# Half of a first MoE layer as seven-product Strassen units, in a kernel of chunked attention followed by a two-layer MoE

## The chip, the cores and the metric

The kernel runs on one core of one Trainium2 chip. The metric is the device time of one execution in microseconds (us). Executions come with the span from first to last instruction, which is about 1.8 us shorter than the time, and with the mean granted clock of the matrix engine (1.0 is full speed). In the text, PE is the matrix engine, PEld its weight loads, DVE the vector engine, ACT the activation engine and POOL the general engine, which here also issues the loads of q, k and v.

## The reference, cut to what matters

```python
def _attn_ref(q, k, v):                  # q, k, v: (8, 8, 576, 64), float32
    # chunks of 64 rows; softmax(q k^T / 8) v inside each chunk
    ...
    return out

def _moe_ref(x, w_in, w_out, beta):      # x: (4608, 512), w_in: (512, 2048), w_out: (2048, 512)
    h = x @ w_in                         # first layer
    g = h * (1.0 / (1.0 + np.exp(-beta * h)))
    return (g @ w_out).astype(np.float32)   # second layer
```

The attention's output, with the heads laid side by side, is the x of the MoE. The kernel computes in 16-bit floats with 32-bit accumulation.

## The kernel before

Tokens go through in nine blocks of 512. Block 0 is treated apart. In the others (1 to 8) the first layer makes sixteen tiles of h ("m-tiles", 128 features by 512 tokens). Each is four matmuls of 128x512 into one PSUM bank, and one Silu on ACT which writes the f16 array `gt`:

```python
    def emit_h(j, m, c0=0, c1=BLK):
        ...
        for n in range(KDM):                      # KDM = 4
            e, z = n // 2, n % 2
            nc.tensor.matmul(
                out=hps_t[j, m][:, c0:c1],
                lhsT=w_r[m // 4][:, 2 * z + e, m // 2 % 2, m % 2, :],
                rhs=xt_t[j][:, n, c0:c1],
                start=(n == 0), stop=(n == KDM - 1),
            )

    def emit_g(j, m):
        hps = hps_t.pop((j, m))
        nc.scalar.activation(
            out=gt_t[j][:, m, :], in_=hps, func=ACTF.Silu,
            scale=beta2[:, m % 2, m // 2:m // 2 + 1],
        )
```

The second layer already is one Strassen step of seven products. Its sums over `gt` (s1 and s2 on DVE, s3 on POOL) are made while the first layer still runs:

```python
    def L1(j, hooks={}, nh=2):
        ...                                       # tiles 0 and 1 first, in two halves
        for m in range(nh, KFF):                  # KFF = 16
            hooks.get(m, lambda: None)()
            emit_m(j, m)                          # emit_h, emit_g
            if j == 0:
                continue
            if m == 8:
                for p in range(4):
                    emit_sum(j, 3, p)             # POOL, needs tiles 0 to 7 only
            if m in (9, 11, 13, 15):
                p = (m - 9) // 2
                fill.extend([lambda w=w, p=p: emit_sum(j, w, p) for w in (1, 2)])
            if m >= 10 and j > 1:
                dve()                             # takes one sum from fill
        hooks.get(KFF, lambda: None)()            # the next block's first scores
```

The steps of the second layer (`mm`) are mixed with the next block's attention (`at`) and with transposes of later q and k (`tr`). At the end of a block POOL is given the loads of a later block, so they run in the following block's first layer:

```python
            mm[5]()
            if j < NB - 1:
                cC()
            go(tr)
            mm[6]()                               # ends with a PSUM copy on ACT and an add on POOL
            if j + 2 < B:
                load_v(j + 2)                     # four loads issued by POOL
            if j + 3 < B:
                load_qk(j + 3)                    # two more
```

Once, before block 1, the weights w_out are scaled and four combinations of them (`tw`) are formed on POOL:

```python
        scale_w_out(0)
        scale_w_out(1)
        for f in T_items(1):                      # transposes of q and k
            f()
        scale_w_out(2)
        scale_w_out(3)
        emit_tw(1)
        emit_tw(2)
        load_v(2)
        load_qk(3)
        emit_tw(4)
        emit_tw(3)
```

Each engine takes its instructions in the order in which the program lists them, and that order is what this case is about: in e4 below, a changed order on ACT alone takes away a wait of 2.62 us.

The softmax here doesn't subtract the row's maximum and nothing guards it: scores larger than these inputs give would overflow.

## Time and profile before

| | before |
|---|---|
| time, median of 3 (lowest to highest) | 289.00 us (288.88 to 289.02) |
| profiled span, granted clock | 287.1 us, 0.999 |
| block 4: first layer with scores / second layer | 14.70 / 14.30 us |
| length of blocks 2 to 7 | 28.97 to 29.00 us |

The length of a block here and below runs from the first matmul of its first layer to the first one of the next block's. "First layer" runs up to the first product of the second layer.

The page of the profiled execution gives the span, the busy time of each engine with its share of the span and its number of instructions, the granted clock in tenths for 40 slices, and the chain of waits that ended last:

```profile
span 287.1 us, 7722 instructions
...
PE 271.6 (95%) x3388; PEld 176.4 (61%) x3388; DVE 140.6 (49%) x261; ACT 161.8 (56%) x240; POOL 117.1 (41%) x114
...
PEclk9999999999999999999999999999999999999999
...
PE 82%; DMA 10%; DVE 3%; POOL 2%; issue 1%; ACT 1%; DVEq 0%; POOLq 0%; ACTq 0%
...
```

PE is busy 95% of the time at full clock, and 82% of the chain is PE. The timeline of PE for one steady block (block 4) gives start, duration, engine, line of the program, operation, output and inputs, shapes and count; a bracket would give idle time before the group and who ended it:

```profile
...
141.39 14.12 PE L240 MATMUL hps<-xt,wi 128*128 128x256 f16 x72
155.44 0.71 PE L155 MATMUL sc<-qT,kT 32*64 32x64 f16 x64
156.09 1.92 PE L310 MATMUL oA<-w_out,gt 128*128 128x256 f16 x16
...
170.39 1.80 PE L240 MATMUL hps<-xt,wi 128*128 128x256 f16 x14
```

There is no bracket: from 141.39 to 170.39 us PE goes from one product to the next. ACT in the same block:

```profile
...
142.24 1.28 ACT L250 ACT_TABLE_LOAD   x1
143.53 3.21 ACT L250 ACTIVATE gt<-hps,beta 128x512 f16<-128x512 f32 x5
...
```

ACT loads the table of the Silu, then does the first five Silus, which had piled up, in one go. POOL in the same block:

```profile
...
143.52 3.44 POOL L95 DMA_DIRECT2D vb<-in_v_dram  x4
...
147.61 0.77 POOL L85 DMA_DIRECT2D ku<-in_k_dram  x1
148.33 4.73 POOL L274 TENSOR_TENSOR s<-gt 128x512 f16<-128x512 f16 x4
```

POOL issues six loads from 143.52 us on, and only after the last of them, at 148.33, starts the sums s3: 4.81 us. Nothing on PE waits for this. The windows view gives for each stretch its length, the busy time of PE, PEld, DVE, ACT and POOL (instructions in brackets), the granted clock, and the DMA's share and rate:

```profile
...
core 0: us, PE busy (x) PEld busy (x) DVE busy (x) ACT busy (x) POOL busy (x), PEclk, DMA share, GB/s
141.39:156.09 14.70, 14.70 (x139) 7.48 (x136) 5.17 (x8) 12.40 (x18) 10.77 (x11) 1.00 1.19 160
156.09:170.39 14.30, 14.30 (x249) 12.05 (x242) 10.61 (x20) 5.26 (x9) 1.27 (x1) 1.00 0.37 74
...
```

In the first layer PE has no free time, ACT is busy 12.40 of 14.70 us, POOL 10.77 and DVE 5.17.

### The profile page before, as it was taken

The page shows a single profiled execution, that of the slowest core. Times are in us where ns is not written, and L with a number is a line of the kernel's source. Part 1 is how long each engine was busy: PE and PEld are TensorE (multiplying, and loading weights), DVE is VectorE, ACT ScalarE, POOL GpSimd, SP SyncE. Part 2 cuts the span into 40 slices and gives each one's busy share as a digit, 9 for nine tenths or more (in the row PEclk, how much of TensorE's full clock was granted, in tenths as well). Part 3 has the DMA queues.
Part 4 walks back from the last instruction along what each step waited for, and adds up shares of the span by engine and source line. Part 5 has one row for each costly group of instructions (what it writes and reads, how often), then busy time and mean ns, then how long its engine had stood idle before and what let it go on. Part 6 is the DMA issues. An engine that isn't in the chain of part 4 may idle for free.

```text
span 287.1 us, 7722 instructions
## 1 busy us (share of the span) xinstructions
PE 271.6 (95%) x3388; PEld 176.4 (61%) x3388; DVE 140.6 (49%) x261; ACT 161.8 (56%) x240; POOL 117.1 (41%) x114
## 2 busy tenths in 40 slices
PE   2779978999999999999999999999999999999995
PEld 0454434546874688468845884588458845885584
DVE  2751483837770677067806680668055404540433
ACT  2249505688348833883388438842884288518710
POOL 8733266994049203920393039302910260016100
PEclk9999999999999999999999999999999999999999
DMA  6999998990239626972597259823902320242013
GB/s 112 177 206 212 211 182 153 184 211 3 75 110 158 130 67 112 159 132 63 105 161 142 59 99 164 154 59 94 154 4 57 94 73 2 57 94 73 2 37 110
DMA packets 69584, 31.95 MB, mean 111 GB/s; under 512 B 53680, under 2 KB 63920, under 8 KB 69552
## 3 DMA queue, kind: packets, MB, share of 16 engines
q0 software_dynamic: 44960, 18.35, 51.9%
q1 hardware_dynamic: 24448, 12.99, 17.4%
q8 instruction: 26, 0.43, 0.6%
q10 hardware_dynamic: 144, 0.13, 0.1%
q14 instruction: 6, 0.05, 0.1%
HBM read 36.71 MB, written 9.44 MB: 161 GB/s over the span
## 4 chain that ended last, share of the span: by engine, by line
PE 82%; DMA 10%; DVE 3%; POOL 2%; issue 1%; ACT 1%; DVEq 0%; POOLq 0%; ACTq 0%
PE hps L240 39%; PE oA L310 20%; DMA ku<-in_k_dram 7%; PE oD L310 5%; PE oB L310 5%; PE oC L310 5%; PE sc L155 4%; PE x L183 3%; DMA vb<-in_v_dram 3%; PE ops L405 1%; DVE kT L127 1%; DVE w_out L118 1%; POOL qu L85 1%; PE oE L310 1%; POOL vb L95 1%
## 5 line engine op out<-in xcount | busy, mean ns | idle before, releaser
L240 PE MATMUL hps<-xt,wi 128*128 128x512 f16 (+1 forms) x656 | 127.8, 353 | 1.2 <-DMA wi<-in_moe_w_in_dram 0.7
L250 ACT ACTIVATE gt<-hps,beta 128x512 f16<-128x512 f32 x144 | 95.8, 688 | 17.8 <-PE hps L240 17.1
L240 PEld LDWEIGHTS <-wi 128*128 128x128 f16 x656 | 63.4, 98 | 61.7 <-DMA xt<-x 1.5
L270 DVE TENSOR_TENSOR s<-gt 128x512 f16<-128x512 f16 x32 | 17.7, 552 | 80.1 <-ACT gt L250 79.9
L355 POOL TENSOR_TENSOR w<-u,u 128x512 f32<-128x512 f32 x7 | 8.9, 1270 | 103.3 <-ACT u L321 103.3
L310 PEld LDWEIGHTS <-s 128*128 128x128 f16 x496 | 46.8, 98 | 6.0
L310 PE MATMUL oA<-tw,s 128*128 128x256 f16 x368 | 44.1, 273 | 0.0
L274 POOL TENSOR_TENSOR s<-gt 128x512 f16<-128x512 f16 x32 | 37.5, 1228 | 4.8 <-ACT gt L250 4.8
L310 PEld LDWEIGHTS <-gt 128*128 128x128 f16 x384 | 36.4, 98 | 4.8
L321 ACT COPY u<-oA 128x512 f32<-128x512 f32 x24 | 14.1, 588 | 37.0 <-PE oA L310 37.0
L164 ACT ACTIVATE et<-sc 128x512 f16<-128x512 f32 x34 | 18.5, 595 | 22.3 <-PE sc L155 22.2
L95 POOL DMA_DIRECT2D vb<-in_v_dram x32 | 27.5, 879 | 6.6 <-DMA wi<-in_moe_w_in_dram 5.0
L200 DVE TENSOR_TENSOR x<-x,rd 128x512 f16<-128x512 f32 x34 | 23.5, 691 | 1.3
L127 DVE STREAM_TRANSPOSE qT<-qu 128x576 f32<-128x576 f32 x16 | 20.0, 1250 | 5.8 <-DMA qu<-in_q_dram 5.8
L127 DVE STREAM_TRANSPOSE kT<-ku 128x576 f32<-128x576 f32 x16 | 19.9, 1241 | 2.1 <-DMA ku<-in_k_dram 2.0
L155 PEld LDWEIGHTS <-kT 32*64 32x64 f16 x1152 | 11.6, 111 | 12.2 <-DVE kT L127 6.3
L155 PE MATMUL sc<-qT,kT 32*64 32x64 f16 x1088 | 12.8, 195 | 6.2 <-DVE kT L127 5.4
L272 DVE TENSOR_TENSOR s<-s,gt 128x512 f16<-128x512 f16 x32 | 17.8, 555 | 1.1
L372 ACT COPY o<-oA 128x512 f32<-128x512 f32 x7 | 4.1, 586 | 23.2 <-PE oA L310 23.2
L405 PE MATMUL ops<-w_out,gt 128*128 128x512 f16 x64 | 15.3, 379 | 1.5 <-DVE w_out L118 1.5
L375 POOL TENSOR_TENSOR o<-t,o 128x512 f32<-128x512 f32 x7 | 8.9, 1270 | 18.0 <-ACT o L372 18.0
L164 ACT ACT_TABLE_LOAD x8 | 10.3, 1283 | 10.0 <-PE sc L155 9.9
(56 smaller groups left out, 208.8 us busy)
## 6 DMA issues: line engine op xcount, KB each, us to landing
out_dram<-osb SPq DMA_DIRECT2D x21, 256.0 KB, 2.2
vb<-in_v_dram POOLq DMA_DIRECT2D x32, 144.0 KB, 4.9
qu<-in_q_dram POOLq DMA_DIRECT2D x7, 576.0 KB, 9.1
ku<-in_k_dram POOLq DMA_DIRECT2D x7, 576.0 KB, 11.1
out_dram<-o SPq DMA_DIRECT2D x14, 256.0 KB, 2.2
wi<-in_moe_w_in_dram POOLq DMA_DIRECT2D x4, 512.0 KB, 12.5
w_out<-in_moe_w_out_dram POOLq DMA_DIRECT2D x4, 512.0 KB, 16.8
qu<-in_q_dram POOLq DMA_DIRECT2D x2, 288.0 KB, 5.3
```

Of the source, the lines that this page charges most:

```text
L95: nc.gpsimd.dma_start(out=t[64 * hp:64 * hp + 64, 2 * z:2 * z + 2, :, 0:D].rearrange("p s c d -> p (s c) d"), in_=v[b, h0:h0 + 2].rearrang ...
L127: nc.vector.transpose(out=dst[b][:, z].rearrange("p t r e -> p (t r e)").bitcast(FP32).rearrange("p (t r) -> p r t", r=RUN), in_=src[b][:, ...
L155: nc.tensor.matmul(out=sc[a % 2][o0:o0 + 64, z, c, :], lhsT=kk[:, cb * CH:(cb + 1) * CH, e], rhs=qq[:, cb * CH:(cb + 1) * CH, e], start=(e ...
L164: nc.scalar.activation(out=et, in_=sc[s], func=ACTF.Exp, scale=scale)
L200: nc.vector.tensor_tensor(out=yy, in0=src, in1=rr.to_broadcast(shape), op=ALU.mult,)
L240: nc.tensor.matmul(out=hps_t[j, m][:, c0:c1], lhsT=w_r[m // 4][:, 2 * z + e, m // 2 % 2, m % 2, :], rhs=xt_t[j][:, n, c0:c1], start=(n == ...
L250: nc.scalar.activation(out=gt_t[j][:, m, :], in_=hps, func=ACTF.Silu, scale=beta2[:, m % 2, m // 2:m // 2 + 1],)
L270: tt(out=s1[:, lo], in0=g[:, lo, dn], in1=g[:, hi, dn], op=ALU.add)
L272: tt(out=s2[:, lo], in0=s1[:, lo], in1=g[:, lo, up], op=ALU.subtract)
L274: tt(out=s3[:, lo], in0=g[:, lo, up], in1=g[:, lo, dn], op=ALU.subtract)
L310: nc.tensor.matmul(out=bank[name][:, i, :], lhsT=a[:, kk, i * 128:(i + 1) * 128], rhs=b[:, kk, :], start=(first and i == 0 and kk == 0), s ...
L405: nc.tensor.matmul(out=ops[t], lhsT=gt_t[j][:, kk, t * 128:(t + 1) * 128], rhs=wo(kk), start=(kk == 0), stop=(kk == KFF - 1),)
```

## The change

The intent is to take matmul time away where PE has no gap. A *unit* makes four of the sixteen m-tiles (2q, 2q+1, 4+2q, 5+2q) by the Strassen-Winograd scheme, with w_in quarters A11..A22 and token-block quarters B11..B22. It has seven products of four 128x256 matmuls: 28 of 256 columns stand for 16 of 512, 12.5% less work. Two units make tiles 0 to 7. Between their products stand the plain tiles 8 to 15 as "spacers", meant to hide the combining of sums. PE accumulates several products in one PSUM bank, so intermediate values are copied out before the next product is added:

- bank A: A11·B11 → copy u1 (ACT); + S2·T2 → copy u2 (DVE); + S3·T3 → copy u3 (DVE); + A22·T4 gives one quarter of the result
- bank C: S1·T1 → copy w1 (DVE); + S4·B22, plus u2 (DVE) gives a second quarter
- bank B: A12·B21, plus u1 (DVE) gives a third
- t = u3 + w1 on POOL gives the fourth

Six Silus then close the unit. The f16 sums T1..T4 of the tokens (`xs`) are made on DVE at the start of every block. The memory for this comes from `gt`, which is left with one buffer. The diff, cut to its core:

```diff
-    gt_p = ctx.enter_context(tc.tile_pool(name="gt", bufs=2))
+    gt_p = ctx.enter_context(tc.tile_pool(name="gt", bufs=1))
...
+    def emit_xs(j):
+        ...
+        tt(out=t[0], in0=b12, in1=b11, op=ALU.subtract)
+        tt(out=t[1], in0=b22, in1=t[0], op=ALU.subtract)
+        tt(out=t[2], in0=b22, in1=b12, op=ALU.subtract)
+        tt(out=t[3], in0=b21, in1=t[1], op=ALU.subtract)
+
+    def unit(j, q, spacers):
+        ...
+        prod("A", a11, b11, True)
+        snap("u1", "A", "a")                      # copy on ACT
+        spacers[0]()
+        prod("A", swr[1], ts[1], False)
+        snap("u2", "A", "v")                      # copy on DVE
+        prod("C", swr[0], ts[0], True)
+        snap("w1", "C", "v")
+        spacers[1]()
+        prod("A", swr[2], ts[2], False)
+        snap("u3", "A", "v")
+        sb["t"] = u_p.tile([128, 2, HT], FP32, tag="t", name="t")
+        nc.gpsimd.tensor_tensor(out=sb["t"], in0=sb["u3"], in1=sb["w1"], op=ALU.add)
+        prod("B", a12, b21, True)
+        nc.vector.tensor_tensor(out=c1[:, :, up_], in0=bank["B"], in1=sb["u1"], op=ALU.add)
+        spacers[2]()
+        prod("A", a22, ts[3], False)
+        prod("C", swr[3], b22, False)
+        nc.vector.tensor_tensor(out=c1[:, :, dn_], in0=bank["C"], in1=sb["u2"], op=ALU.add)
+        for i in range(2):
+            silu(m2 + i, dn_, sb["t"][:, i])
+        for i in range(2):
+            silu(m2 + i, up_, bank["A"][:, i])
+        for i in range(2):
+            silu(m1 + i, slice(0, BLK), c1[:, i])
...
+    def L1(j, hooks={}, first=None):              # blocks 1 to 8
+        ...
+        emit_xs(j)
+        unit(j, 0, [sp(8), sp(9), sp(10)])
+        sp(11)()
+        for p in (0, 2):
+            emit_sum(j, 3, p)
+        unit(j, 1, [sp(12), sp(13), sp(14)])
+        for p in (1, 3):
+            emit_sum(j, 3, p)
+        sp(15)()
...
         scale_w_out(1)
-        for f in T_items(1):
-            f()
+        T1 = T_items(1)
+        T1[0]()
+        T1[1]()
         scale_w_out(2)
+        T1[2]()
+        T1[3]()
         scale_w_out(3)
+        load_v(2)
         emit_tw(1)
+        load_qk(3)
         emit_tw(2)
-        load_v(2)
-        load_qk(3)
```

Left out are the making of the weight sums `sw`, some extra idle matmuls at the start, and a moved hook. In block 1 the four transposes T2 move to tiles 9, 11, 13 and 15.

More of the change, by code (lines that the diff above doesn't have):

```diff
@@ L51 @@
     xt_p = ctx.enter_context(tc.tile_pool(name="xt", bufs=2))
-    gt_p = ctx.enter_context(tc.tile_pool(name="gt", bufs=2))
+    gt_p = ctx.enter_context(tc.tile_pool(name="gt", bufs=1))
     s_p = ctx.enter_context(tc.tile_pool(name="s", bufs=1))
     u_p = ctx.enter_context(tc.tile_pool(name="u", bufs=1))
+    xs_p = ctx.enter_context(tc.tile_pool(name="xs", bufs=1))
+    c_p = ctx.enter_context(tc.tile_pool(name="c", bufs=2))
     osb_p = ctx.enter_context(tc.tile_pool(name="osb", bufs=4))
@@ L70 @@
     tw = [big.tile([128, NM, HM], FP16, name=f"tw{i}") for i in range(4)]
+    sw = [big.tile([128, 2, DFF // 4], FP16, name=f"sw{i}") for i in range(4)]
     NV = 3
@@ L220, in emit_xp, with emit_idle @@
         nc.scalar.copy(out=xt_t[j][:, :, t0:t0 + 128], in_=xps)
-    def emit_idle(n):
+    def emit_idle(n, w=512):
         d = ps_p.tile([128, BLK], FP32, tag="p", name="idle")
         for _ in range(n):
-            nc.tensor.matmul(out=d, lhsT=zero[:, 0:128], rhs=zero, start=True, stop=True)
+            nc.tensor.matmul(
+                out=d[:, 0:w], lhsT=zero[:, 0:128], rhs=zero[:, 0:w], start=True, stop=True)
     gt_t = {}
@@ L253, in emit_g, with emit_sw @@
         )
+    xs_t = {}
+    def emit_sw():
+        s1, s2, s3, s4 = sw
+        a11, a12 = w_in16[0][:, 0::2], w_in16[0][:, 1::2]
+        a21, a22 = w_in16[1][:, 0::2], w_in16[1][:, 1::2]
+        tt = nc.vector.tensor_tensor
+        tt(out=s1, in0=a21, in1=a22, op=ALU.add)
+        tt(out=s2, in0=s1, in1=a11, op=ALU.subtract)
+        tt(out=s3, in0=a11, in1=a21, op=ALU.subtract)
+        tt(out=s4, in0=a12, in1=s2, op=ALU.subtract)
+    def emit_xs(j):
+        x = xt_t[j]
+        b11, b12 = x[:, 0:2, 0:HT], x[:, 0:2, HT:BLK]
+        b21, b22 = x[:, 2:4, 0:HT], x[:, 2:4, HT:BLK]
+        t = xs_t[j] = [xs_p.tile([128, 2, HT], FP16, tag=f"xs{i}", name=f"xs{i}") for i in range(4)]
+        tt = nc.vector.tensor_tensor
+        tt(out=t[0], in0=b12, in1=b11, op=ALU.subtract)
+        tt(out=t[1], in0=b22, in1=t[0], op=ALU.subtract)
+        tt(out=t[2], in0=b22, in1=b12, op=ALU.subtract)
+        tt(out=t[3], in0=b21, in1=t[1], op=ALU.subtract)
@@ new lines, in unit, with prod, snap, silu @@
+    def unit(j, q, spacers):
+        x = xt_t[j]
+        ts = xs_t[j]
+        up_, dn_ = slice(0, HT), slice(HT, BLK)
+        b11, b21, b22 = x[:, 0:2, up_], x[:, 2:4, up_], x[:, 2:4, dn_]
+        swr = [t.rearrange("p k (m i r) -> p k m r i", r=2, i=128) for t in sw]
+        a11, a12, a22 = w_r[0][:, 0::2], w_r[0][:, 1::2], w_r[1][:, 1::2]
+        bank = {"A": ps_s.tile([128, 2, HT], FP32, tag=f"sc{q}", name="wA")}
+        xx = ps_x.tile([128, 2, 2, HT], FP32, tag="x", name="wX")
+        bank["B"], bank["C"] = xx[:, 0], xx[:, 1]
+        sb = {}
+        def prod(b, a, rhs, first):
+            for i in range(2):
+                for kk in range(2):
+                    nc.tensor.matmul(
+                        out=bank[b][:, i, :], lhsT=a[:, kk, q, i, :], rhs=rhs[:, kk, :],
+                        start=(first and i == 0 and kk == 0), stop=(kk == 1),
+                        skip_group_check=True,
+                    )
+        def snap(nm, b, eng):
+            sb[nm] = u_p.tile([128, 2, HT], FP32, tag=nm, name=nm)
+            if eng == "a":
+                nc.scalar.copy(out=sb[nm], in_=bank[b])
+            else:
+                nc.vector.tensor_copy(out=sb[nm], in_=bank[b])
+        def silu(m, cols, src):
+            nc.scalar.activation(
+                out=gt_t[j][:, m, cols], in_=src, func=ACTF.Silu,
+                scale=beta2[:, m % 2, m // 2:m // 2 + 1],
+            )
+        m1, m2 = 2 * q, 4 + 2 * q
+        c1 = c_p.tile([128, 2, BLK], FP32, tag="c1", name="c1")
+        prod("A", a11, b11, True)
[20 more added lines that the diff above has]
+            silu(m2 + i, up_, bank["A"][:, i])
+        for i in range(2):
+            silu(m1 + i, slice(0, BLK), c1[:, i])
@@ L433, in dve, with L1_plain @@
                 fill.pop(0)()
-    def L1(j, hooks={}, nh=2):
+    def L1_plain(j, hooks, nh):
         for m in range(nh):
@@ L442, in L1, with sp, f @@
         for m in range(nh, KFF):
-            hooks.get(m, lambda: None)()
             emit_m(j, m)
-            if j == 0:
-                continue
-            if m == 8:
-                for p in range(4):
-                    emit_sum(j, 3, p)
-            if m in (9, 11, 13, 15):
-                p = (m - 9) // 2
-                fill.extend([lambda w=w, p=p: emit_sum(j, w, p) for w in (1, 2)])
-            if m >= 10 and j > 1:
-                dve()
+    def L1(j, hooks={}, first=None):
+        gt_t[j] = gt_p.tile([128, KFF, BLK], FP16, tag="gt", name="gt")
+        def sp(m):
+            def f():
+                hooks.get(m, lambda: None)()
+                emit_m(j, m)
+            return f
+        if first:
+            first()
+        emit_xs(j)
[7 more added lines that the diff above has]
+        sp(15)()
+        for p in (0, 2, 1, 3):
+            fill.extend([lambda w=w, p=p: emit_sum(j, w, p) for w in (1, 2)])
+        dve(4)
         hooks.get(KFF, lambda: None)()
@@ L500 @@
         emit_pv(1, spare=True, xbar=False)
+        emit_idle(4, 256)
         emit_xp(0)
@@ L504 @@
         emit_pv(3, spare=True, xbar=False)
-        L1(0, {-2: lambda: emit_xp(2), -3: lambda: emit_xp(3)}, 4)
+        L1_plain(0, {-2: lambda: emit_xp(2), -3: lambda: emit_xp(3)}, 4)
+        emit_sw()
         scale_w_out(0)
         scale_w_out(1)
-        for f in T_items(1):
-            f()
+        T1 = T_items(1)
+        T1[0]()
+        T1[1]()
         scale_w_out(2)
+        T1[2]()
+        T1[3]()
         scale_w_out(3)
+        load_v(2)
         emit_tw(1)
+        load_qk(3)
         emit_tw(2)
-        load_v(2)
-        load_qk(3)
         emit_tw(4)
@@ L520 @@
             9: lambda: emit_sc(2),
-            11: lambda: emit_sc(3),
-            12: lambda: emit_pv(4, xbar=False),
+            12: lambda: [emit_pv(4, xbar=False), emit_sc(3)],
             13: lambda: [emit_pv(5, xbar=False), emit_xp(4)],
@@ L537 @@
                 T2 = T_items(2)
-                hooks.update({-1: lambda: emit_xp(7), 4: T2[0], 7: T2[1], 10: T2[2], 12: T2[3]})
-            L1(j, hooks)
+                hooks.update({9: T2[0], 11: T2[1], 13: T2[2], 15: T2[3]})
+            L1(j, hooks, (lambda: emit_xp(7)) if j == 1 else None)
             at = []
```

## The prediction

> **What bounds the kernel now.** PE is 95% busy on the page; the chain of waits is 82% PE. In the timeline the steady token block (141.56 to 170.55 us) is unbroken matmuls: first layer 13.95 us, second layer with attention 15.05. In the first-layer window ACT is busy 11.86 us, DVE 5.00, POOL 10.77.
>
> **What the change removes.** In the chain, 128x512 matmuls cost 218 ns and 128x256 ones 109 ns. A unit replaces 16 of 512 (3.49 us) by 28 of 256 (3.06 us). Two units save 0.86 us per block, 6.9 over eight: 282 us if nothing else changed. Splitting the w_out scaling should remove PE's 1.5 us wait at 41.3 us: about 2 with nearby waits.
>
> **What it adds, per block.** ACT: two copies (0.59 us) and, per unit, four 256-wide Silus where two 512-wide ones stood. [...] DVE: four f16 additions (0.42 us alone), ten PSUM operations (0.69). POOL: two additions (1.27).
>
> **The new chain.** ACT and PE are in order, so I laid each engine's instructions out in issue order with these durations (an estimate; the same layout of the present kernel gives 29.1 us per steady block, trace 28.99). From the first-layer start T:
> 1. ts1 is ready only near T+2.5: DVE transposes until T+1.2, and the f16 additions stretch beside POOL's output addition (0.97 to 1.26 us in this trace[...]). PE waits about 1.3 us in unit 0.
> 2. t of unit 0 queues on POOL behind the v, q and k load issues, until T+6.9, and ends near T+8.1. ACT waits for it, then runs six Silus and tile 11's before unit 1's u1 copy, near T+12.2. Unit 1's second product may not overwrite that bank before: PE waits about 3 us (2 in blocks without loads).
> 3. The scores then wait for A's Silus, the second layer for the last c1 Silu: 1.4 us.
>
> Net: 5.8 us of waits less 1.4 us of saved or absorbed PE work: +4.3 us in blocks 2 to 5, +3 in 6 to 8. In block 1 the four 4.1 us POOL subtractions for tw run until about 58 us and hold up the f16 additions: +4 to +7. The single g buffer costs nothing: its readers end before the next Silu. Sum: +31, less 2 for w_out.
>
> **Prediction:** 319 us, 306 to 329 eight times in ten. Faster by over 2%: 0.03; within 2%: 0.03; slower by over 2%: 0.94.
>
> **What would show it.** PE busy falls to about 85%. The timeline shows one PE gap of 2 to 3.5 us per block ended by ACT u1 in unit 1, one near 1 us ended by DVE ts and smaller ones before scores and the second layer. First-layer windows are 17 to 19 us, second-layer ones stay 15. The POOL t additions start right after load issues.
>
> **What would make it wrong.** t issued earlier than the loads, half Silus much faster than estimated, or unblocked DVE additions: then the loss shrinks towards 290. If gaps slow later matmuls, worse than 329.

Its sum is +31 less 2 on the 289 us of before, which was put at 319. The trace of before has no 256-wide Silu, and of the additions only their times, 0.97 and 1.26 us beside POOL's sums and 0.41 to 0.43 after them (block 4). The steps to T+12.2 and to the wait of about 3 us used the cut time and stand as the author's estimate, and "half Silus much faster than estimated" refers to it.

## The result, and the profile after

| | before | after |
|---|---|---|
| time, median (lowest to highest) | 288.98 us (288.88 to 289.02) | 333.38 us (330.97 to 333.98) |
| ratio of after to before, 95% interval | | 1.152 (1.146 to 1.158), slower |
| profiled span, granted clock | 287.1 us, 0.999 | 332.2 us, 0.974 |
| first layer / second layer (block 4 before, block 3 after) | 14.70 / 14.30 us | 20.73 / 14.57 us |

A ratio is the mean time of one kernel's fast runs over that of the other's fast runs of the same rounds, so it is not quite the ratio of the medians. All four runs of after spread by 3 us with the clock: 330.97 us at 0.984, 333.98 at 0.974.

The prediction had the direction and the place right. Its range ended at 329, 4.4 us short of the median. The page after:

```profile
span 332.2 us, 8211 instructions
...
PE 278.7 (84%) x3520; PEld 191.1 (58%) x3520; DVE 222.5 (67%) x377; ACT 170.8 (51%) x288; POOL 139.9 (42%) x130
...
PEclk9999999599999899989999999799999999999999
...
PE 40%; ACT 15%; DMA 14%; POOL 14%; DVE 10%; issue 5%; POOLq 0%; DVEq 0%
...
```

PE is busy 84% of the span instead of 95%, and its share of the chain is 40% instead of 82%. ACT, POOL and DVE now hold 39% of it together. In the clock line four slices show 5, 8, 8 and 7 where all showed 9 before. PE in block 3 (it starts at 128.51 us; `wA` and `wX` are products of a unit, `hps` those of a plain tile):

```profile
...
129.48 1.04 PE L244 MATMUL hps<-xt,wi 128*128 128x512 f16 x4 [0.36 <-DMA xt<-x]
131.44 0.61 PE L297 MATMUL wA<-xs,sw 128*128 128x256 f16 x4 [0.93 <-DVE xs L278]
...
137.10 1.03 PE L244 MATMUL hps<-xt,wi 128*128 128x512 f16 x4
140.74 1.01 PE L297 MATMUL wA<-xs,sw 128*128 128x256 f16 x4 [2.62 <-ACT u L306]
...
142.40 1.91 PE L244 MATMUL hps<-xt,wi 128*128 128x512 f16 x4
...
148.61 0.70 PE L158 MATMUL sc<-qT,kT 32*64 32x64 f16 x63 [0.68 <-ACT gt L311]
149.24 2.19 PE L398 MATMUL oA<-w_out,gt 128*128 128x256 f16 x16
...
```

There are four waits of PE: 0.36 us for the transposed tokens, 0.93 for the sums `xs`, 2.62 in unit 1 for the copy u1 on ACT, and 0.68 before the scores for a Silu. After the 2.62 the same four matmuls take 1.01 instead of 0.61 us, and a plain tile 1.91 instead of 1.03. ACT in the same stretch, around the 2.62 us:

```profile
...
136.79 0.91 ACT L311 ACTIVATE gt<-t,beta 128x256 f16<-128x256 f32 x2 [0.98 <-POOL t L329]
137.60 0.82 ACT L311 ACTIVATE gt<-wA,beta 128x256 f16<-128x256 f32 x2
138.32 1.32 ACT L311 ACTIVATE gt<-c,beta 128x512 f16<-128x512 f32 x2
139.54 0.68 ACT L254 ACTIVATE gt<-hps,beta 128x512 f16<-128x512 f32 x1
140.11 0.58 ACT L306 COPY u<-wA 128x512 f32<-128x512 f32 x1
...
```

ACT waits 0.98 us for POOL's t, then does the six Silus of unit 0 and the one of tile 11, and only then the copy u1 of unit 1, at 140.11. PE had finished tile 12 at 138.13 and starts again at 140.74. And POOL:

```profile
...
130.59 3.44 POOL L98 DMA_DIRECT2D vb<-in_v_dram  x4
...
134.69 0.76 POOL L88 DMA_DIRECT2D ku<-in_k_dram  x1
135.41 1.34 POOL L329 TENSOR_TENSOR t<-u,w 128x512 f32<-128x512 f32 x1
...
```

t stands in the queue behind the six load issues. The last one takes 0.76 us from 134.69, and t starts at 135.41. The whole chain is there: loads on POOL, then t, then seven Silus on ACT, then u1, then PE. The windows of block 3:

```profile
...
128.51:149.24 20.73, 16.15 (x155) 9.69 (x152) 11.66 (x20) 12.60 (x23) 10.91 (x11) 0.92 0.86 116
149.24:163.81 14.57, 14.47 (x249) 11.99 (x242) 13.15 (x22) 6.22 (x10) 3.96 (x3) 1.00 0.30 69
...
```

The second layer is nearly unchanged (14.57 to 14.30 us), the first is 6.03 us longer. ACT is busy 12.60 us, no more than 0.20 above before. Its instructions are not too many; they come too late.

Block 1 has another wait. DVE there, when it makes the first two token sums, and POOL, which forms the last three combinations `tw`:

```profile
...
54.33 2.40 DVE L277 TENSOR_TENSOR xs<-xt 128x512 f16<-128x512 f16 x1 [0.18 <-ACT xt L223]
56.77 4.15 DVE L278 TENSOR_TENSOR xs<-xt,xs 128x512 f16<-128x512 f16 x1
...
```

```profile
...
48.23 8.22 POOL L372 TENSOR_TENSOR tw<-w_out,tw 128x2048 f16<-128x2048 f16 x2
56.41 4.23 POOL L372 TENSOR_TENSOR tw<-w_out 128x2048 f16<-128x2048 f16 x1
...
```

The first f16 subtraction takes 2.40 us and the second 4.15. Each ends just after one of POOL's 4.1 us subtractions ends (56.45 and 60.64); the next two, when POOL is done, take 0.41. PE waits 5.60 us for them.

The lengths of the blocks, by first-layer starts in the timeline of PE:

| block | 1 | 2 | 3 | 4 | 5 | 6 | 7 | 8 to the end |
|---|---|---|---|---|---|---|---|---|
| before | 29.49 | 28.99 | 28.97 | 29.00 | 28.97 | 28.99 | 28.98 | 29.77 |
| after | 39.98 | 35.02 | 35.30 | 33.60 | 34.97 | 32.80 | 32.79 | 34.23 |
| more | 10.49 | 6.03 | 6.33 | 4.60 | 6.00 | 3.81 | 3.81 | 4.46 |

Block 1 starts 0.43 us earlier than before (53.51 to 53.94). So the 45.1 us of longer span are these eight sums less 0.43.

### The profile page after: what moved, and what is told of

Read it like the earlier page. It is cut to its first block, busy times and chain, and to the rows that moved or that the text cites. A ratio compares the mean times of both kernels' runs of the same rounds, so it can differ in the third digit from the quotient of the medians.

```text
span 332.2 us, 8211 instructions
## 1 busy us (share of the span) xinstructions
PE 278.7 (84%) x3520; PEld 191.1 (58%) x3520; DVE 222.5 (67%) x377; ACT 170.8 (51%) x288; POOL 139.9 (42%) x130
## 3 DMA queue, kind: packets, MB, share of 16 engines
q0 software_dynamic: 44960, 18.35, 45.1%
## 4 chain that ended last, share of the span: by engine, by line
PE 40%; ACT 15%; DMA 14%; POOL 14%; DVE 10%; issue 5%; POOLq 0%; DVEq 0%
PE oA L398 14%; ACT gt L311 11%; DMA w_out<-in_moe_w_out_dram 10%; POOL t L329 5%; PE hps L244 5%; PE oD L398 4%; PE oB L398 4%; PE wA L297 4%; POOL vb L98 4%; DMA ku<-in_k_dram 2%; PE wX L297 2%; DMA xt<-x 2%; DVE u L308 2%; PE x L186 2%; DVE xs L277 2%
## 5 line engine op out<-in xcount | busy, mean ns | idle before, releaser
L244 PE MATMUL hps<-xt,wi 128*128 128x512 f16 (+1 forms) x336 | 83.7, 380 | 6.3 <-DMA xt<-x 5.2
L254 ACT ACTIVATE gt<-hps,beta 128x512 f16<-128x512 f32 x80 | 54.2, 687 | 46.1 <-PE hps L244 46.0
L362 POOL TENSOR_TENSOR s<-gt 128x512 f16<-128x512 f16 x32 | 39.5, 1254 | 47.6 <-ACT gt L311 47.6
L244 PEld LDWEIGHTS <-wi 128*128 128x128 f16 x336 | 33.0, 100 | 32.6 <-DMA xt<-x 7.2
L308 DVE COPY u<-wA 128x512 f32<-128x512 f32 x32 | 22.1, 691 | 43.5 <-PE wA L297 42.8
L297 PEld LDWEIGHTS <-sw 128*128 128x128 f16 x256 | 25.9, 104 | 42.2 <-issue 20.9
L297 PE MATMUL wA<-xs,sw 128*128 128x256 f16 x128 | 21.5, 295 | 26.8 <-ACT u L306 16.6
L329 POOL TENSOR_TENSOR t<-u,w 128x512 f32<-128x512 f32 x16 | 20.6, 1286 | 34.9 <-DVE u L308 34.9
L167 ACT ACTIVATE et<-sc 128x512 f16<-128x512 f32 x34 | 18.5, 594 | 18.0 <-PE sc L158 17.9
L158 PE MATMUL sc<-qT,kT 32*64 32x64 f16 x1088 | 14.2, 195 | 11.7 <-DVE kT L130 6.5
L297 PEld LDWEIGHTS <-wi 128*128 128x128 f16 x192 | 19.1, 100 | 8.0 <-issue 0.4
L358 DVE TENSOR_TENSOR s<-gt 128x512 f16<-128x512 f16 x32 | 21.0, 657 | 3.7 <-ACT gt L311 3.7
L158 PEld LDWEIGHTS <-kT 32*64 32x64 f16 x1152 | 12.2, 111 | 18.1 <-issue 8.9
```

Of the source, the lines that this page charges most:

```text
L158: nc.tensor.matmul(out=sc[a % 2][o0:o0 + 64, z, c, :], lhsT=kk[:, cb * CH:(cb + 1) * CH, e], rhs=qq[:, cb * CH:(cb + 1) * CH, e], start=(e ...
L244: nc.tensor.matmul(out=hps_t[j, m][:, c0:c1], lhsT=w_r[m // 4][:, 2 * z + e, m // 2 % 2, m % 2, :], rhs=xt_t[j][:, n, c0:c1], start=(n == ...
L254: nc.scalar.activation(out=gt_t[j][:, m, :], in_=hps, func=ACTF.Silu, scale=beta2[:, m % 2, m // 2:m // 2 + 1],)
L297: nc.tensor.matmul(out=bank[b][:, i, :], lhsT=a[:, kk, q, i, :], rhs=rhs[:, kk, :], start=(first and i == 0 and kk == 0), stop=(kk == 1), ...
L308: nc.vector.tensor_copy(out=sb[nm], in_=bank[b])
L329: nc.gpsimd.tensor_tensor(out=sb["t"], in0=sb["u3"], in1=sb["w1"], op=ALU.add)
```

## The experiments

**Theory.** Two things together. First, the order of the queues: in each block t waits behind the loads on POOL, unit 0's Silus wait for t on ACT, u1 of unit 1 waits behind the Silus, and PE waits for u1. Second, the clock: a wait of that length makes the following matmuls run at half speed for a while (in block 3 a plain tile takes 1.91 us behind the 2.62 us, and 1.03 before it).

**Rivals.** (a) ACT has too little capacity for the half-wide Silus and copies. (b) The single `gt` buffer holds things up. (c) The half clock comes from the traffic of the loads and not from the wait. (d) Units cannot gain here, whatever the order.

Each run computed the right result. Runs were made in four batches, each on one chip and with its own runs of the kernel before; the medians of those were 288.66 to 288.82 us. In the batch of e9, e10 and e11 one run of the kernel before was slow (403.42 us at a clock of 0.664) and is not used. Edits are shown against the kernel after, unless said otherwise.

### Is the clock part of the loss? e2_keep_busy

Idle matmuls into a spare bank fill the wait in unit 1 of each block (eight) and in unit 0 of block 1 (22). They do no useful work.

```diff
         spacers[0]()
+        if q == 1:
+            emit_idle(8)
+        elif j == 1:
+            emit_idle(22)
         prod("A", swr[1], ts[1], False)
```

> The changed kernel with work added and no wait removed: dummy matmuls on zeros (8 of 512 columns) in PE's gap before the second product of unit 1 in every block, and 22 in the 5.6 us gap of unit 0 in block 1. Theory [...]: the dummies fill 1.7 of the 1.8 to 2.6 us gaps, the granted clock goes back to about 1.0 in the span before the end, every wait stays where it was: 7 us less, 326 us, 324 to 328, with 180 more matmuls. Rival (the lower clock comes from load, or the half-speed matmuls cost nothing because PE waits anyway): the clock stays at 0.974 or the time stays at 331 to 335.

Measured: 327.68 us (327.07 to 328.04), ratio 1.135 (1.132 to 1.138). The clock by core of this run (span and mean granted clock; after had 332.2 us and 0.974):

```profile
...
core 0: 325.6 us, clock 0.998
...
```

Adding matmuls made the kernel 5.7 us faster. Blocks 1 to 7 became shorter by 1.46, 1.41, 1.70, 0, 1.37, 0 and 0 us, which makes 5.9. The clock records of after have half-clock spells in blocks 1, 2, 3 and 5 and in no other (beside the last 0.3 us of the span), the same four that gained here. The spells last 3.41 us (twice that in block 1), 17.07 us in all. In blocks 2, 3 and 5 the wait in unit 1 is 2.6 us, and in block 1 the wait in unit 0 is 5.60; in block 4 the waits are 2.05 (for xt) and 1.86, in blocks 6 to 8 the wait in unit 1 is 1.79, and there is no spell.

The clock records of after also say where such a wait lay. The time between two changes of the clock is a whole multiple of 3.41 us there (40.96, 30.72, 64.85 and 119.47 us at full clock, 3.41 and 6.83 at half), so the changes lie on a grid. Adding up PE's idle time (matmul ends are modelled in the trace) in every 3.41 us stretch of that grid at full clock, from the first clock record at 14.5 us on, the half clock followed each of the four stretches with 2.02 us or more and none with 1.80 us or less. Block 3's wait of 2.62 us lies whole in one stretch, and block 4's wait of 2.05 us lies across two (0.26 and 1.79). So in this trace the place of a wait counts beside its length; e7 below has the clearest pair.

### Do the loads make the wait, and do they make the half clock? e6_loads_after_t and e1_loads_early

In e6 POOL is given the loads only after t of unit 0:

```diff
         nc.gpsimd.tensor_tensor(out=sb["t"], in0=sb["u3"], in1=sb["w1"], op=ALU.add)
+        if q == 0 and j > 1:
+            if j + 1 < B:
+                load_v(j + 1)
+            if j + 2 < B:
+                load_qk(j + 2)
...
             mm[6]()
-            if j + 2 < B:
-                load_v(j + 2)
-            if j + 3 < B:
-                load_qk(j + 3)
```

> The other way to take the loads from in front of t: POOL issues them straight after unit 0's t, in the first layer of the next block. Theory (the loads in front of t cost what the first order test was meant to show, and that test failed only because their transfers then ran together with the transposing transfers of xt): xt lands within 2 to 4 us as in the changed kernel, t of unit 0 ends near T+7, PE's wait in unit 1 is 1.8 us in every block from 2 on, blocks 2 to 5 last about 32.8 us, the half-clock spells in blocks 2 to 5 go: 323 us, 320 to 327. Rival (the loads' place is of no account for t, and the first test was slower for another reason than the transfers): 331 or more.

Measured: 326.58 us (325.94 to 329.28), ratio 1.133 (1.127 to 1.138). Blocks 2, 3 and 5 are 32.80 us, exactly what 6 and 7 were in after; block 4, which waits 1.79 us for xt, is 33.26. PE at unit 1 of block 2 in this run:

```profile
...
105.00 0.60 PE L297 MATMUL wA<-xs,sw 128*128 128x256 f16 x4 [1.79 <-ACT u L306]
...
```

The wait is 1.79 us, and the product after it takes its normal 0.60. The loads are still in the first layer, with the same traffic, only later in it; there is no half clock after block 1. Rival (c) falls: with the traffic kept and the waits shorter, the spells are gone. It also shows what the loads cost in the queue: 2.6 less 1.8 us in the wait itself, and the spell on top.

In e1 the same loads were moved earlier, into the second layer of the block before:

```diff
             cB()
+            if j + 2 < B:
+                load_v(j + 2)
+            if j + 3 < B:
+                load_qk(j + 3)
             go(at)
...
             mm[6]()
-            if j + 2 < B:
-                load_v(j + 2)
-            if j + 3 < B:
-                load_qk(j + 3)
```

> The changed kernel with one move: the v, q and k loads are issued by POOL in the middle of the second layer (where POOL idles over 8 us) and no longer at its end. Theory (queue order: t waits on POOL behind the loads, ACT waits for t in order, PE waits for ACT's u1 copy; the half-clock spells follow from those waits): t of unit 0 ends near T+7 in blocks 2 to 5 too, PE's wait in unit 1 there falls from 2.6 us to the 1.8 us of blocks 6 to 8, all blocks from 2 on last about 32.8 us, and the three half-clock spells at 107, 141 and 209 us go[...]. About 5 us of waits and 5 us of clock: 323 us, 320 to 327. Rival (ACT simply has too much work): ACT's work is the same, so nothing moves by more than 2 us: 331 to 334.

Measured: 353.32 us (352.59 to 356.14), ratio 1.227 (1.221 to 1.233). This was a miss. PE at the start of block 2 and at its unit 1:

```profile
...
99.84 1.04 PE L297 MATMUL wA<-xt,wi 128*128 128x256 f16 x4 [6.91 <-DMA xt<-x]
...
112.34 0.60 PE L297 MATMUL wA<-xs,sw 128*128 128x256 f16 x4 [1.79 <-ACT u L306]
...
```

The unit wait fell to 1.79 us as expected. But PE now waits 6.91 us for xt, the transposed tokens. They travel by DMA too. From issue to landing they take, in after and then in this run:

```profile
...
DMA to landing us min/median/max: 2.4/2.7/4.1
```

```profile
...
DMA to landing us min/median/max: 6.1/7.4/8.2
```

Instead of a median of 2.7 us they take 7.4 beside the loads, though SP issues them and POOL the loads. The tuned kernel had placed its loads where no transpose travels (in block 4 of before the loads are issued from 143.5 us on and the last lands at about 159; the transposes are issued at 139.9, landing in 2.4 us, and again from 161.4 on), and my expectation had not asked for that.

### Is it the order on ACT, or ACT's capacity? e4_defer_silus

The six Silus of unit 0 are issued after u1 of unit 1. No work is added or removed.

```diff
-    def unit(j, q, spacers):
+    def unit(j, q, spacers, late=None):
...
         snap("u1", "A", "a")
+        if late:
+            late()                                # the six Silus of unit 0
         spacers[0]()
...
-        unit(j, 0, [sp(8), sp(9), sp(10)])
+        late = unit(j, 0, [sp(8), sp(9), sp(10)])
         sp(11)()
-        for p in (0, 2):
-            emit_sum(j, 3, p)
-        unit(j, 1, [sp(12), sp(13), sp(14)])
-        for p in (1, 3):
+        unit(j, 1, [sp(12), sp(13), sp(14)], late)
+        for p in (0, 2, 1, 3):
             emit_sum(j, 3, p)
```

> The changed kernel with the same ACT work in another order: unit 0's six Silus are issued after unit 1's u1 copy and no longer before it. Theory (ACT's in-order queue and not its load is what PE waits for): the wait ended by ACT's u1 in unit 1 is gone in every block, late t from the loads no longer reaches PE, blocks fall to about 31 us (waits for ts1 and before the scores and the second layer stay, the latter longer by 0.5), no half-clock spell from block 2 on: 16 us of waits and 5 of clock, 312 us, 307 to 318. Rival (ACT has too much work): Silus end at the same time, the wait moves to the scores and the second layer in full, 328 to 334.

Measured: 313.84 us (312.73 to 314.63), ratio 1.087 (1.083 to 1.091). PE in block 3, at unit 1 and before the scores, and the window of that first layer:

```profile
...
132.06 0.60 PE L297 MATMUL wA<-xs,sw 128*128 128x256 f16 x4
...
138.29 0.70 PE L158 MATMUL sc<-qT,kT 32*64 32x64 f16 x63 [0.71 <-ACT gt L311]
...
```

```profile
...
122.50:138.92 16.42, 14.41 (x154) 9.05 (x152) 11.63 (x18) 12.38 (x23) 11.00 (x11) 1.00 1.08 146
...
```

Where the wait of 2.62 us stood there is none. The first layer is 16.42 us instead of 20.73, with ACT busy 12.38 us: the same ACT work in a window 4.3 us shorter. Rival (a) falls. The steady blocks are 31.0 us. Against the 33.60 of e2, which has the wait but the full clock, that is 2.6 us less in the blocks with loads; against the 32.79 of the last blocks it is 1.8 less. Both are the sizes of the wait. What still stands between 31.0 and 29.0 are the waits for xt (0.37), `xs` (0.92) and before the scores (0.71), and small ones in the second layer (14.6 instead of 14.3 us), each with the short hand-off that is estimated in point 3 below, less the 0.86 us of saved work.

### Is u1 itself the matter? e3_u1_on_dve

The copy u1 goes to DVE, where no Silu stands before it.

```diff
-        snap("u1", "A", "a")
+        snap("u1", "A", "v")
```

> The changed kernel with one word changed: u1 of both units is copied by DVE and no longer by ACT. Theory (PE waits for whatever stands before u1 in an in-order queue): the wait ended by ACT's u1 in unit 1 goes in every block; in unit 0 u1 now stands behind the four f16 additions and the last transpose, so PE's wait before the second product there grows from 0.9 to about 2.4 us, ended by the u1 copy on DVE. Net 1.5 us less per block in blocks 2 to 5 and little in 6 to 8, the half-clock spells of blocks 2 to 5 go or move to unit 0: 323 us, 318 to 330. Rival (ACT's extra work and not its order is what PE waits for): the gap in unit 1 stays ended by another ACT instruction, 330 or more.

Measured: 330.2 us as the median of four runs, of which two were slow (331.67 and 331.69) and two fast (326.34 and 328.72). By the fast ones the ratio is 1.134 (1.130 to 1.138). The profiled run was one of the slow ones, so only the place of its waits is read. PE in unit 0 of one block:

```profile
...
130.54 1.01 PE L297 MATMUL wA<-xs,sw 128*128 128x256 f16 x4 [2.18 <-DVE u L308]
...
```

The wait in unit 1 is gone, as expected. In its stead unit 0 now waits 2.18 us for DVE's u1, which stands behind DVE's transposes and f16 sums, and the product behind it takes 1.01 us. So the clock falls again, in the fast runs too: their mean clocks are 0.973 and 0.969. The time was too uncertain to weigh this to a microsecond. It shows that a wait moved from one queue to another is not a wait removed.

### What do the other parts cost? e7_block1_plain, e5_plain_first_layer and e11_plain_two_g

In e7 block 1 alone has the plain first layer of before, with its transposes T2 in their old places:

```diff
-                hooks.update({9: T2[0], 11: T2[1], 13: T2[2], 15: T2[3]})
-            L1(j, hooks, (lambda: emit_xp(7)) if j == 1 else None)
+                hooks.update({-1: lambda: emit_xp(7), 4: T2[0], 7: T2[1], 10: T2[2], 12: T2[3]})
+            (L1_sums if j == 1 else L1)(j, hooks)     # L1_sums is the loop of before
```

> The changed kernel with the plain first layer in block 1 alone, where POOL still runs the tw subtractions; units from block 2 on. Theory (block 1 loses 11 us because two f16 additions on DVE stand behind 4.1 us POOL subtractions, 5.6 us, with a half-clock spell of about 2.5 us after it, and the later waits of a unit block): block 1 falls from 40.2 us to about 29, all others stay: 322 us, 319 to 325. Rival (block 1 is slow by its start and not by its units, so that the loss stays): 330 or more.

Measured: 321.96 us (320.71 to 322.67), ratio 1.114 (1.111 to 1.118). Block 1 is 29.60 us instead of 39.98, the others stay as in after. Block 1 alone cost 10.4 us. This trace also has two equal waits with different ends, the first in block 3 and the second in block 4:

```profile
...
129.17 0.76 PE L297 MATMUL wA<-xs,sw 128*128 128x256 f16 x4 [2.61 <-ACT u L306]
...
130.57 1.91 PE L244 MATMUL hps<-xt,wi 128*128 128x512 f16 x4
...
164.47 0.60 PE L297 MATMUL wA<-xs,sw 128*128 128x256 f16 x4 [2.61 <-ACT u L306]
...
```

The first lies whole in one stretch of the 3.41 us grid (126.06 to 129.47), and the half clock begins at 129.47, within the product that takes 0.76 us. The second lies across the border at 163.60 (1.75 us before it, 0.86 after), and there is no half clock: the product takes its 0.60.

In e5 every block has the plain first layer, and everything else of the change is kept: the single `gt` buffer, the order of the w_out scaling and of the first loads.

```diff
     def L1(j, hooks={}, first=None):
-        gt_t[j] = gt_p.tile([128, KFF, BLK], FP16, tag="gt", name="gt")
...                                               # emit_xs, both units and their sums taken out
+        for m in range(2, KFF):
+            sp(m)()
+            ...                                   # sums as before
```

> The changed kernel with the plain first layer in every block and all the rest of the change kept (one g buffer, w_out scaling between transposes, the loads' new place before tw, sw computed and not used). Theory (the seven-product units cost all of it; one g buffer costs nothing and the new w_out order saves what shows at the first first-layer start, 0.7 us): 288.3 us, 287 to 289.5. Rival (a large part of the 44 us comes from the single g buffer, which stops the first layer of a block from overlapping the second layer of the one before): well over 292 us.

Measured: 289.45 us (289.16 to 290.01), ratio 1.003 (1.001 to 1.005). So all but 1 us of the loss belongs to the units. Its steady blocks are 29.17 us, 0.19 more than before. In e11 the only further edit is the second buffer:

```diff
-    gt_p = ctx.enter_context(tc.tile_pool(name="gt", bufs=1))
+    gt_p = ctx.enter_context(tc.tile_pool(name="gt", bufs=2))
```

> The plain first-layer run with two g buffers: what is left of the change is the w_out order, the loads before tw and the unused sw. Theory (the single g buffer costs 0.18 us a block through the table load's wait; the new w_out order gains about 1 us before the first layer of block 1): blocks of 28.99 us, 287.9 us, 287.3 to 288.4. Rival (the 0.18 us came from elsewhere in the change): blocks of 29.18 us, 289.2 to 289.8.

Measured: 287.89 us (287.48 to 288.45), ratio 0.998 (0.9965 to 0.9996). The blocks are back at 28.98 us. ACT at the start of a block in e5, then in e11:

```profile
...
171.11 1.28 ACT L254 ACT_TABLE_LOAD   x1 [0.91 <-PE hps L244]
```

```profile
...
169.95 1.28 ACT L254 ACT_TABLE_LOAD   x1
...
```

With one buffer the Silu may not write `gt` until the second layer's last products have read it. The table load in front of the Silu starts 0.91 us later, when the first tile is done; with two buffers it starts at once behind the copy. Rival (b) is real but small: 0.19 us a block, about 1.5 in eight.

### Can units gain at all? e8_reordered_units, e9_one_unit, e10_one_unit_two_g and e12_one_unit_low_first

For e8 I kept both units and changed the order: two plain tiles first so that the `xs` sums get time, u1 on DVE, unit 0's Silus right behind unit 0, unit 1's Silus in the second layer, whose first product is one that does not need them; and block 1 plain.

```diff
-        emit_xs(j)
-        unit(j, 0, [sp(8), sp(9), sp(10)])
-        sp(11)()
+        for m in (8, 9):
+            emit_h(j, m, 0, HT)
+        for m in (8, 9):
+            emit_h(j, m, HT, BLK)
+            emit_g(j, m)
+        emit_xs(j, 0)                             # T1, T2; the others later, in unit 0
+        a0, t0, c0 = unit(j, 0, [sp(10), sp(11), sp(12)])
+        a0()
+        t0()
...
+        a1, t1, c1_ = unit(j, 1, [sp13, sp(14), sp(15)])   # sp13: tile 13, then c0
...
+            if tr and j > 1:
+                hooks[13] = tr.pop(0)             # one transpose of q moved into the first layer
```

> An attempt to keep the seven-product units in blocks 2 to 8 and hide their tails: two plain tiles open each block, u1 is copied by DVE, the f16 additions are spread, Silus of units stand between those of plain tiles, the second layer opens with the products that need plain tiles only, its exp comes after the units' Silus, one transpose moves into the first layer, block 1 plain. Theory (order and not work is what the change lacks; ACT has about 13 us of work per first layer and 8 us to spare in the second layer): blocks 2 to 8 last 28.2 to 29.0 us, clock 1.0: 285 us, 282 to 290. Rival (the added ACT and DVE work doesn't fit under PE at any order): blocks of 30 us or more, 297 us or more.

Measured: 314.97 us (314.30 to 315.59), ratio 1.091 (1.089 to 1.094). A miss by 30 us, and the larger part of it came from my own last edit. DVE in the first layer of one block:

```profile
...
198.80 1.26 DVE L130 STREAM_TRANSPOSE qT<-qu 128x576 f32<-128x576 f32 x1 [3.03 <-DMA qu<-in_q_dram]
...
```

The transpose of q that I moved forward waits for the load of q, and stands in front of unit 1's copy u2. PE waits for that copy 3.98, 3.70, 1.58 and 2.91 us in the four blocks with such a load, and behind the three longer waits half-clock spells follow, 13.65 us in all: some 19 of the 30 us (an estimate that counts half of a spell as lost). In blocks 6 and 7, which have no such load, the length is 30.24 and 29.86 us, still above before's 28.98: the second layer, which in this order contains the scores, takes 16.06 us, and before's, counted with its scores, takes about 15.0 (14.30 and 0.7). Two units in this order do not pay even without the slip.

For e9 I kept a single unit (tiles 0, 1, 4, 5) and made the twelve others plain, three of them (8, 9, 10) first; block 1 plain. As in e8, u1 goes to DVE and the `xs` sums are spread.

```diff
+        for m in (8, 9, 10):
+            emit_h(j, m, 0, HT)
...
+        s_a, s_t, s_c = unit(j, 0, [sp(11), sp(12), sp(13)])
+        sp(2)()
+        s_t()
+        sp(3)()
+        s_a()
+        for p in (1,):
+            emit_sum(j, 3, p)
+        sp(6)()
+        s_c(0)
+        sp(7)()
+        s_c(1)
+        for p in (0, 2, 3):
+            emit_sum(j, 3, p)
+        sp(14)()
+        sp(15)()
```

> One seven-product unit per block in blocks 2 to 8, in the middle of the first layer: three plain tiles before it, three as spacers, six after it with the unit's Silus between theirs; u1 copied by DVE; loads, second layer and transposes where the kernel before has them; one g buffer; block 1 plain. Theory (PE's saving is real, 0.43 us per unit, and only the order hid it): blocks last 29.18 us of the plain first-layer run less 0.43, so 28.75, and the kernel 286.4 us, 285 to 288, under the plain first-layer run's 289.45. Rival (a unit cannot gain at any order, as its half-width products or its extra reads and writes slow PE by as much): blocks of 29.2 us or more, 289.5 us or more.

Measured: 294.90 us (294.58 to 296.17), ratio 1.023 (1.021 to 1.025). A miss, but a useful one. The e10 run has the same order and two `gt` buffers, with smaller weight sums and one `c1` buffer to make room:

```diff
-    gt_p = ctx.enter_context(tc.tile_pool(name="gt", bufs=1))
+    gt_p = ctx.enter_context(tc.tile_pool(name="gt", bufs=2))
-    c_p = ctx.enter_context(tc.tile_pool(name="c", bufs=2))
+    c_p = ctx.enter_context(tc.tile_pool(name="c", bufs=1))
-    sw = [big.tile([128, 2, DFF // 4], FP16, name=f"sw{i}") for i in range(4)]
+    sw = [big.tile([128, 2, DFF // 8], FP16, name=f"sw{i}") for i in range(4)]
```

> The one-unit kernel with two g buffers again (the half of sw that one unit needs, and one c buffer, make the room). Theory (in the plain first-layer run the single g buffer cost 0.18 us a block: the Silu table load waits there for the first tile, 0.9 us later than in the kernel before, and tiles queue up behind it): the table load comes straight after the output copy, blocks last 28.55 us: 285 us, 283.5 to 287, some 1.4 us under the one-unit run. Rival (the 0.18 us came from elsewhere): same as the one-unit run within 0.5 us.

Measured: 294.90 us (294.35 to 294.97), ratio 1.022 (1.020 to 1.023). Another miss, so the buffer was not the matter in e9. In the blocks 2 to 4 the first layer of e10 is 14.26 us where before has 14.69: the 0.43 us of one unit, all of it. But the second layer is 15.4 us instead of 14.3. PE in the second layer of one block of e10:

```profile
...
196.03 0.32 PE L186 MATMUL x<-vb,et 64*64 64x65 f16 x16 [0.51 <-DVE x L203]
...
```

PE waits for DVE's attention work (0.51 us here, 0.17 before the group of `x` ahead of it), which stands behind the sums s1 and s2. In the plain kernel s3 starts on POOL as soon as tiles 0 to 7 are there, and DVE's sums follow tile by tile. In e10, as in e9, tiles 2, 3, 6 and 7 and the unit's Silus come late. So three of POOL's four s3 subtractions run from 186.80 to 190.78 us, after the start of the second layer, and the DVE sums beside them take 1.26 to 1.37 us instead of 0.42.

For e12 only the order of the tiles changes against e10: tiles 2, 3 and 6 first, the unit with spacers 7, 8 and 9, its Silus right behind, and the upper tiles last, as in before.

```diff
-        for m in (8, 9, 10):
+        for m in (2, 3, 6):
...
-        s_a, s_t, s_c = unit(j, 0, [sp(11), sp(12), sp(13)])
-        sp(2)()
-        s_t()
-        sp(3)()
+        s_a, s_t, s_c = unit(j, 0, [sp(7), sp(8), sp(9)])
         s_a()
-        for p in (1,):
+        s_t()
+        for p in (1, 3, 2):
             emit_sum(j, 3, p)
-        sp(6)()
+        sp(10)()
         s_c(0)
-        sp(7)()
+        sp(11)()
         s_c(1)
-        for p in (0, 2, 3):
-            emit_sum(j, 3, p)
-        sp(14)()
-        sp(15)()
+        emit_sum(j, 3, 0)
+        for m in range(12, 16):
+            sp(m)()
```

> The one-unit kernel with two g buffers and another order of tiles: the other tiles of the lower half (2, 3, 6, 7) come before and in the unit, the upper half after it, and the unit's six Silus directly behind it. In the first one-unit runs the first layer did get 0.43 us shorter (14.26 against 14.69 us) but the second layer 1.2 us longer, as the sums on POOL and DVE came later, ran beside each other and held up the attention additions on DVE. Theory (with the sums early again the second layer is back at 14.3 us): blocks of 28.6 us and 285 us, 283.5 to 287.5. Rival (the unit's extra DVE and ACT work costs the second layer its 1.2 us at any order): 293 to 295.

Measured: 287.09 us (286.40 to 288.06), ratio 0.995 (0.992 to 0.997). The windows of block 3, first and second layer:

```profile
...
110.92:125.18 14.26, 14.26 (x155) 9.13 (x152) 9.45 (x15) 11.68 (x20) 12.07 (x12) 1.00 1.22 162
125.18:139.48 14.30, 14.30 (x249) 12.06 (x242) 11.73 (x24) 5.42 (x9) 1.27 (x1) 1.00 0.33 75
...
```

PE is busy the whole time again, at full clock, and the block is 28.56 us against 28.97 before. The unit's saving has arrived and the second layer is at its old 14.30 us. POOL's first three s3 subtractions now end in the first layer, at 122.73 us, and seven of the eight DVE sums take 0.41 to 0.43 us each. The version is faster than before and after, by half a per cent: within 2% it counts as the same, but its interval lies below one. Of the 2.3 us by which its span is shorter than before's (284.8 to 287.1), 1.07 come before block 1, 0.7 from blocks 1 to 7 and 0.5 from the last. The first of these lies before any unit runs, and e11, which has no unit, is also below before. Against e11's 287.89 us, measured in another batch, the unit is worth about 0.8 us in the whole kernel; its sure sign is the block, 28.56 us against e11's 28.98. Blocks 5 to 7 gave part of it back in waits for xt of 0.89, 0.25 and 0.16 us. Rival (d) falls for one unit. For two it stays open: no order that I ran made two units pay.

## Why the prediction was right or wrong

**Right: the mechanism and its place.** The prediction laid each engine's queue out in order and named the chain of loads, t, Silus, u1 and PE. It had t starting at T+6.9, and it started at 135.41 with T = 128.51. It had a PE wait of "about 3 us (2 in blocks without loads)", and it was 2.6 (1.8). PE busy was to fall to about 85% and fell to 84%; PE's wait for `xs` was to be 1.3 us and was 0.93, with 0.36 for xt before it (the stretched f16 additions that the prediction quotes from before, 0.97 to 1.26 us, ran there beside POOL's sums s3; in after the first of the four did stretch beside POOL's output addition, to 1.23 us in block 3, and the others took 0.42); the second layer was to stay as it was. Per block, without the clock, this gives 4.6 us in blocks 2 to 5 (6.03 less the 1.41 that e2 returned in block 2), against 4.3 predicted. That these are so near is in part luck: the waits in block 3 are 4.9 us (0.36, 0.93, 2.62, 0.68, and 0.27 in the second layer) where the prediction had 5.8, and the work saved is 0.86 where it had 1.4 saved or absorbed. The half Silu, whose estimate is cut above, was measured in block 3: two of them took 0.91 and 0.82 us. e4 and e6 show the chain by taking single links out.

**Wrong: the sum.** It came to about 30 us (5.5 for block 1 as the middle of its range, four times 4.3, three times 3, less 2) and the span grew by 45.1. The missing 15.4 us are in these terms:

| term, as the prediction put it | predicted, us | measured, us | short by | shown by |
|---|---|---|---|---|
| "If gaps slow later matmuls, worse than 329" | 0 in the sum | 5.9 | 5.9 | e2, and the clock records |
| block 1, "+4 to +7" | 5.5 | 9.0, and 1.5 of clock counted above | 3.5 | block lengths, e2, e7 |
| blocks 6 to 8, "+3" | 9 | 12.1 | 3.1 | block lengths |
| w_out split, "less 2" | −2 | −0.4 | 1.6 | starts of block 1 |
| blocks 2 to 5, "+4.3" | 17.2 | 18.5, without clock | 1.3 | block lengths, e2 |

1. *The clock.* This is the step that failed. I named it as a risk and gave it no size, though the waits that I predicted, 3 us and more, were as long as the ones that set it off (2.6 and 5.60). With its 5.9 us in the sum the estimate would have been 325, and a range as wide around it would have held the result; e2, in which this term alone is gone, took 327.68 us. How many of the waits set off a spell differs from run to run: by their mean clocks (0.984 of 329.2 us, 0.974 of 332.2) the fastest of the four runs of after had some three stretches of 3.41 us at half clock and the slowest five (an estimate from these numbers), and the slowest took 3 us more.
2. *Block 1.* The prediction had POOL's subtractions end at about 58 us; they ended at 60.64. DVE's second sum ended 0.28 us after that and PE waited 5.60 us. Behind it there came the ordinary wait in unit 1 (1.54), and one of 0.88 before the scores. What the moved transposes T2 between DVE's copies add to that, I have not separated.
3. *Blocks without loads.* The wait in unit 1 was 1.79, under the predicted 2, and yet the blocks were 3.8 us longer and not 3. In block 7 the waits are 0.38, 0.90, 1.79 and 0.67 us, the second layer's first product takes 2.19 us instead of 1.92, and 0.86 us of work is saved: 3.15 us. The other 0.66 can be estimated from the same timeline: with no wait behind it, a product gives way to the next 0.44 us after its start, and before a wait it counts for its full 0.60, so each of the four waits costs some 0.16 us beyond itself. No run separated them.
4. *The w_out scaling.* Block 1 started 0.43 us earlier in after. In the profiles of the experiments, in which the program up to there is the same or nearly so, it started at 52.3 to 53.7 us, so the gain over the 53.94 of before is between 0.2 and 1.7 us, and never the 2 of the prediction.
5. *"The single g buffer costs nothing."* It cost 0.19 us a block in the plain kernel (e5 against e11). The products that read `gt` do end before the next Silu; the table load in front of that Silu was overlooked. In the table this sits inside the lines for the blocks, and whether it is the same 0.19 with units was not measured.

The saving itself, 0.43 us for each unit, was as estimated (e12). It was real from the start, and after the change PE was no longer what the time depended on.

## What to carry to other kernels

When PE has no gap, an edit that saves matmuls but ties each product to copies, sums and activations on other engines has to be laid out queue by queue, with every instruction that already stands in those queues (loads, table loads, transposes) in its place; here the one unit that kept all queues in order brought its full 0.43 us a block, and two units that did not cost 3.8 to 6.3 us a block in blocks 2 to 8. A wait in PE can bring the half clock behind it, which cost about 1.4 to 1.7 us a block here (e2): in after 2.02 us of idle time in one stretch of the 3.41 us grid did so and 1.80 us did not, and in e7 a wait of 2.61 us went either way by where it lay. So it should be priced as a risk, and it is worth a run with idle matmuls in the gap to learn that share. Before moving loads to an idle stretch of the issuing engine, look at what else travels by DMA at that time: in e1 the transposes beside the loads took 7.4 us to land instead of 2.7.
